# The first gate and value weights ordered behind the first blocks' values, and the whole schedule searched anew

## The chip, the cores and the metric

One core of a Trainium2 chip. The time is the device time of one execution in microseconds, of which the profile's span covers the instructions. The engines go by their profile names: PE (matrix), PEld (its weight loads), ACT (scalar), DVE (vector), POOL (GpSimd) and SP (sync, which here only issues loads and stores).

## The reference, cut to what matters

Sparse attention over four batches, then a gated feed-forward layer over the 3072 rows.

```python
# q, k, v: (4, 8 heads, 768, 64); chunks of 32 keys, the 6 best per row
ub = sum(maximum(q * k_min, q * k_max))        # bound of each chunk
sel = the 6 chunks of largest ub among the causal ones
attn = softmax(where(sel & causal, q @ k.T / 8, -1e9)) @ v
x = attn as (3072, 512)
out = (sigmoid(x @ w_gate) * (x @ w_val)) @ w_out   # 512 -> 1536 -> 512
```

In the first 128 rows of a batch there are at most four causal chunks, so nothing has to be chosen there.

## The kernel before, in words

The rows are cut into eight units of three blocks of 128 rows. Unit 0 holds the first blocks of batches 0, 1 and 2, which need no choice of chunks; the first block of batch 3 goes with unit 2. For every unit u the operations have names:

- `first` (unit 0 and the block of batch 3): loads `kf`, `qf` (two halves each, L575) and `vf` (L570); transposes `kfT`, `qfT` (L648), casts `kf16`, `qf16`; scores `scf` (L685); exponentials `expf` on ACT (L690); the causal mask `cmf` on POOL (L692); products with the values `pvf` (L699); reciprocal and scaling `rzf`, `xf` (L705, L707); transposes `xpsf` (L714) and copies `xTf` into the transposed rows `xT`. The values are cast as `v16_0_0` (batch 0, L612) or `vc_1`, `vc_2`. `vf1` sets the ones column.
- `keys_wide`, `queries_wide` (units 1 and 2): loads `k0..k3`, `q0..q3` (L586), copies `kn`, `qn`, transposes `kT`, `qT` (L734), extremes `kx` (L620), copies `hk`, `hq`, positive parts `qm` (L636 on DVE or POOL, L634 on ACT). Later units take keys and queries in blocks.
- `choose`: bounds `ub` (L835), then on DVE the transposes, the eight largest and the mask that the scores add.
- `attend`: scores `sc` (L896), exponentials (L907), causal mask `cm` on POOL (L913), products with the values `pv` (L929), `rz`, `x`, `xps`, `xT`.
- `ffn`: for each of twelve column blocks a gate product `g` and a value product `v` (four matmuls each, L1078), tanh on ACT (L1087), their product `hg` on DVE (L1091); for units 0 to 3 the output products `o0`, `o1`, `o2` (L1119), copied and stored; units 4 to 7 use seven products of sums (`p`, L1013) instead.

The weights come as nine loads issued on POOL, each a third of a matrix, which convert from 32 to 16 bits:

```python
def weights(i, prio, after):
    lo, hi = 512 * i, 512 * i + 512
    return plan.add(f"wg{i}", {POOL: (760, 760)}, lambda e: nc.gpsimd.dma_start(wg16[:, :, lo:hi], wgs[:, :, lo:hi]),
             reads=after, writes=[("wg", i)], prio=prio, dma=(3000, 2048)), ...   # the same for wv{i}
```

`weights_out` does so for `wo0..wo2` (L557). Gate blocks 0 to 3 need `wg0`, 4 to 7 `wg1`, 8 to 11 `wg2`; the values likewise; `o0` needs `wo0` and so on.

The order of the work is written out. A table ORDER lists all 1826 operations with their engine, found by a search outside the kernel, and a table SLOTS gives each of 991 buffers its place. The kernel walks ORDER and emits each operation on the engine named; each engine then works off its own queue in that order:

```python
for w in ORDER.split():
    name, _, e = w.partition("=")
    op.engine = {"P": PE, "A": ACT, "V": DVE, "G": POOL, "S": SP}[e]
    assert op.engine in op.engines and all(d in done for d, _ in op.deps), name
```

The dependencies in the plan (`reads`, `writes`) bind the search and are asserted here. The waits of the program come from the tiles that an instruction touches.

Of the kernel before, what the change touches and what calls it, by code (L numbers as in the profile page):

```python
# [96 lines left out]
epat0=V ident=G vf1_2=G epat=G v10=G ident16=V kcr0=V kf0_0=S hkp000=A k2_u1=S kn_u1_2=V kT_u1_2=P kx1_u1_2=V hkp011=V vf1_1=G  # L97
hkp001=G kf1_0=S kfT_0=P kf16_0=V kt_u1_2=A hkp010=V hk1_u1_2=V ap0=V hkp100=V qf0_0=S qf1_0=S qfT_0=P qf16_0=A kf1_1=S kf0_1=S
kfT_1=P kf16_1=A scf_0=P expf_0_0=A qf0_1=S qf1_1=S qfT_1=P qf16_1=A scf_1=P k0_u1=S wg0=G expf_0_1=A cmf_0_1=G vf_0=S v16_0_0=G
pvf_0_1=P kx0_u1_2=V rzf_0_1=V xf_0_1=V kn_u1_0=A kT_u1_0=P qf1_2=S kf0_2=S qf0_2=S kf1_2=S kfT_2=P hq0=V kf16_2=V expf_1_0=A  # L100
cmf_1_0=G qfT_2=P qf16_2=A cmf_0_0=G pvf_0_0=P rzf_0_0=V xf_0_0=V vf_1=S vc_1=G xpsf_0_1=P pvf_1_0=P rzf_1_0=V expf_1_1=A
cmf_1_1=G wv0=G scf_2=P expf_2_0=A cmf_2_0=G xTf_0_1=A xpsf_0_0=P xf_1_0=V xpsf_1_0=P kxf0=V pvf_1_1=P rzf_1_1=V xf_1_1=V
xpsf_1_1=P kxf1=V expf_2_1=A kt_u1_0=A vf_2=S cmf_2_1=G vc_2=A pvf_2_1=P rzf_2_1=V xf_2_1=V pvf_2_0=P rzf_2_0=V xf_2_0=V k1_u1=S
kn_u1_1=A kT_u1_1=P xTf_1_0=V xTf_1_1=V xpsf_2_1=P xTf_2_1=V kx1_u1_0=V q0_u1=S qn_u1_0=A qT_u1_0=P xpsf_2_0=P q1_u1=S qn_u1_1=A
qT_u1_1=P q2_u1=S kt_u1_1=A qn_u1_2=A qT_u1_2=P wv1=G wg1=G wv2=G k3_u1=S kn_u1_3=A kT_u1_3=P hk1_u1_0=A xTf_0_0=V qf_u1_1=V
xTf_2_0=A g_u0_2=P qf_u1_0=A qf_u1_2=A hkp110=A q3_u1=S hk0_u1_1=G kcr_f=G hkf0=G hk1_u1_1=G qn_u1_3=G qm_u1_0=A qT_u1_3=P
qm_u1_2=A qf_u1_3=A hk0_u1_2=G kx1_u1_1=V ap1=V kx0_u1_0=V kx0_u1_1=V hq0_u1_1=G wg2=G hq0_u1_2=G qm_u1_1=V kx1_u1_3=V kx0_u1_3=V
kt_u1_3=V g_u0_3=P g_u0_0=P g_u0_1=P hq0_u1_0=V kcr_u1=V v_u0_3=P qm_u1_3=A tanh_u0_2=A tanh_u0_0=A tanh_u0_3=A v_u0_2=P hg_u0_2=V
hkf1=V v_u0_0=P hg_u0_0=V hq0_u1_3=G wo0=G hk0_u1_3=G ub_u1=P ubn0_u1=V ubm0_u1=V mx0_u1=V ubn1_u1=V ap0_u1=V apt0_u1=V
hqm0_u1_0=G wo1=G hkp101=A hk1_u1_3=A hkp111=A tanh_u0_1=A hk0_u1_0=A v_u0_5=P v_u0_4=P v_u0_7=P hg_u0_3=V kcr1=V v_u0_1=P  # L110
hg_u0_1=V hqm0_u1_2=A g_u0_5=P tanh_u0_5=A hg_u0_5=V hq1=V g_u0_7=P tanh_u0_7=A hg_u0_7=V hq1_u1_3=V ubm1_u1=V sc_u1_3_2=P
sc_u1_2_2=P sc_u1_3_1=P exp_u1_3_2=A exp_u1_2_2=A g_u0_4=P tanh_u0_4=A hg_u0_4=V mx1_u1=V ap1_u1=V hq1_u1_1=V apt1_u1=V
sc_u1_0_2=P sc_u1_0_1=P exp_u1_0_2=A exp_u1_0_1=A sc_u1_1_1=P exp_u1_1_1=A sc_u1_2_1=P exp_u1_2_1=A sc_u1_2_0=P sc_u1_1_0=P
hq1_u1_0=G hq1_u1_2=G g_u0_6=P tanh_u0_6=A sc_u1_1_2=P exp_u1_2_0=A cm_u1_2=G wo2=G sc_u1_3_0=P exp_u1_3_0=A sc_u1_0_0=P
exp_u1_0_0=A exp_u1_3_1=A v_u0_8=P v_u0_9=P v_u0_6=P hg_u0_6=V hqm1_u1_0=V g_u0_9=P tanh_u0_9=A g_u0_8=P g_u0_10=P tanh_u0_10=A
g_u0_11=P tanh_u0_11=A exp_u1_1_0=A exp_u1_1_2=A v_u0_10=P hg_u0_10=V o0_u0_0=P v_0_3=S v_0_1=S v16_0_3=G cm_u1_3=G v16_0_1=G
hqm1_u1_2=G v_0_2=S v16_0_2=G pv_u1_2=P hg_u0_9=V pv_u1_3=P rz_u1_1=V x_u1_1=V tanh_u0_8=A hg_u0_8=V sc_u1_4_2=P exp_u1_4_2=A
# [4 lines left out]
o1_u0_0=P o2_u0_0=P k1_u2=S k2_u2=S kn_u2_2=V kT_u2_2=P kx1_u2_2=V kt_u2_2=V q0_u2=S qn_u2_0=A kt_u2_0=A xT_u1_0=A kn_u2_1=A
qT_u2_0=P qf_u2_0=A osb_u0_0=A cm_u1_7=G pv_u1_7=P pv_u1_6=P q3_u2=S qn_u2_3=G qT_u2_3=P rz_u1_3=V x_u1_3=V kT_u2_1=P pv_u1_5=P
cm_u1_4=G pv_u1_4=P kf0_3=S k3_u2=S kn_u2_3=G kT_u2_3=P q1_u2=S qn_u2_1=A hq0_u2_0=G hk1_u2_0=G qm_u2_2=G hq0_u2_2=G xps_u1_3=P
qT_u2_1=P o1_u0_1=P kx0_u2_2=V rz_u1_2=V x_u1_2=V kx1_u2_1=V xps_u1_2=P qf1_3=S kf1_3=S kfT_3=P qm_u2_0=A qf_u2_3=A hq0_u2_3=G
# [1132 lines left out]
```

## Time and profile before

| | us |
|---|---|
| median of 3 runs | 290.59 (290.22 to 292.78) |
| the profiled execution | 291.15 |
| its span | 289.4 |
| PE busy in it | 272.8 |
| DVE, ACT, POOL busy | 213.6, 186.9, 147.0 |

The mean granted clock of PE is 0.982 over the span. A row of the timeline gives start, length, engine, line, operation, what it writes and reads, how many, and in brackets the idle time ahead of it with what ended it. "DMA to landing" is the time from a load's issue to its data being there, lowest, median and highest of the loads asked for.

### The profile page before, as it was taken

What the parts mean: (1) busy time and instruction counts of PE and PEld (TensorE: products, weight loads), DVE (VectorE), ACT (ScalarE), POOL (GpSimd) and SP (SyncE); (2) the same over time, 40 slices, a digit from 0 to 9 for tenths busy, and PEclk for the clock granted to TensorE, in tenths of its full rate; (3) what the DMA queues carried; (4) which work ended last, traced back from release to release, by engine and by line L of the source; (5) the groups of instructions that cost most, each with busy time, mean ns of one, the idle gap of its engine ahead of it and who ended that gap; (6) DMA issues with size and microseconds to landing.
All of it is one profiled execution on the core that took longest, in us unless ns stands there. A gap on an engine that the chain in (4) does not pass through costs nothing.

```text
span 289.4 us, 7287 instructions
## 1 busy us (share of the span) xinstructions
PE 272.8 (94%) x2764; PEld 187.3 (65%) x2764; DVE 213.6 (74%) x613; ACT 186.9 (65%) x394; POOL 147.0 (51%) x233
## 2 busy tenths in 40 slices
PE   2478999999999999999999999999999999999994
...
GB/s 161 199 264 215 211 212 205 174 194 155 182 259 163 104 181 81 91 155 201 219 198 89 37 76 38 2 0 2 2 76 1 0 2 0 111 0 111 0 0 146
DMA packets 123378, 32.70 MB, mean 113 GB/s; under 512 B 111440, under 2 KB 120400, under 8 KB 123344
## 3 DMA queue, kind: packets, MB, share of 16 engines
...
q14 instruction: 13, 0.11, 0.1%
HBM read 30.67 MB, written 6.29 MB: 128 GB/s over the span
## 4 chain that ended last, share of the span: by engine, by line
PE 81%; DMA 8%; DVE 4%; POOL 2%; SPq 1%; issue 1%; ACT 0%; DVEq 0%; POOLq 0%; ACTq 0%
PE v_u L1078 19%; PE g_u L1078 18%; PE sc_u L896 11%; PE o_u L1119 10%; PE p_u L1013 8%; PE pv_u L929 7%; DMA wo<-in_moe_w_out_dram 6%; PE ube_u L835 2%; PE xps_u L956 2%; SPq L575 1%; DMA kf<-in_k_dram 1%; PE kfT L648 1%; DMA kq_u<-in_k_dram 1%; PE qT_u L734 1%; DVE ox L1030 1%
## 5 line engine op out<-in xcount | busy, mean ns | idle before, releaser
L907 ACT ACTIVATE att_u<-sc_u 128x512 f16<-128x512 f32 (+3 forms) x184 | 86.7, 579 | 8.9 <-PE sc_u L896 8.1
L1087 ACT ACTIVATE gate_u<-g_u 128x384 f16<-128x384 f32 x96 | 46.3, 500 | 55.7 <-PE g_u L1078 40.2
L1091 DVE SCALAR_TENSOR_TENSOR hg_u<-gate_u,v_u 128x384 f16<-128x384 f16 x96 | 50.9, 546 | 35.6 <-PE v_u L1078 29.0
L1078 PE MATMUL g_u<-xT_u,wg 128*128 128x384 f16 x384 | 73.7, 328 | 0.7 <-DMA wg<-in_moe_w_gate_dram 0.7
L1078 PE MATMUL v_u<-xT_u,wv 128*128 128x384 f16 x384 | 72.1, 326 | 0.0
L1078 PEld LDWEIGHTS <-wv 128*128 128x128 f16 x384 | 36.6, 98 | 22.7 <-issue 0.5
L1078 PEld LDWEIGHTS <-wg 128*128 128x128 f16 x384 | 36.3, 98 | 23.1 <-DMA wg<-in_moe_w_gate_dram 1.5
L913 POOL TENSOR_SCALAR_AFFINE_SELECT att_u<-att_u 128x384 f16<-128x384 f16 (+1 forms) x56 | 28.3, 510 | 41.1 <-ACT att_u L907 40.3
L1119 PE MATMUL o_u<-wo,hg_u 128*128 128x512 f16 x144 | 34.0, 379 | 0.1
L929 PE MATMUL pv_u<-v,att_u 128*128 128x65 f16 x640 | 26.5, 193 | 0.0
L929 PEld LDWEIGHTS <-att_u 128*128 128x128 f16 x640 | 24.1, 97 | 2.2 <-issue 0.6
L896 PE MATMUL sc_u<-hqe,hke 128*128 128x128 f16 (+2 forms) x220 | 24.3, 243 | 0.2 <-POOL hqe L411 0.2
L896 PE MATMUL sc_u<-hqo,hko 128*128 128x128 f16 (+2 forms) x220 | 24.3, 243 | 0.0
L1119 PEld LDWEIGHTS <-hg_u 128*128 128x128 f16 x144 | 13.8, 98 | 14.4 <-DMA wo<-in_moe_w_out_dram 0.5
L896 PEld LDWEIGHTS <-hke 128*128 128x128 f16 x220 | 16.4, 98 | 5.1 <-ACT osb_u L1128 0.6
L896 PEld LDWEIGHTS <-hko 128*128 128x128 f16 x220 | 16.5, 98 | 3.9
L612 POOL CAST v<-v 128x512 f16<-128x512 f32 x23 | 14.5, 637 | 3.1 <-PE pv_u L929 2.3
L948 DVE TENSOR_TENSOR x_u<-pv_u,rz_u 128x384 f16<-128x384 f32 (+1 forms) x28 | 14.7, 529 | 0.7
L1030 DVE SCALAR_TENSOR_TENSOR sw<-p_u,sw 128x256 f32<-128x256 f32 (+1 forms) x20 | 10.6, 531 | 5.8 <-PE p_u L1013 3.4
L1000 POOL TENSOR_TENSOR sw<-hg_u 128x256 f16<-128x256 f16 x5 | 3.3, 669 | 18.4 <-DVE hg_u L1091 18.4
L858 DVE MAX8 mx_u<-ubn_u 128x8 f32<-128x8 f32 (+16 forms) x152 | 12.4, 162 | 0.2
L636 POOL TENSOR_SCALAR qm_u<-qf_u 128x768 f32<-128x768 f32 (+2 forms) x6 | 11.4, 1894 | 0.3
...
## 6 DMA issues: line engine op xcount, KB each, us to landing
...
wo<-in_moe_w_out_dram POOLq DMA_DIRECT2D x3, 512.0 KB, 13.5
```

The lines of the kernel that those rows point to most:

```text
L612: plan.add(f"v16_{b}_{ib}", {POOL: pool(H * D)}, lambda e: nc.gpsimd.tensor_copy(v16[b % 2][:, ib, :, 0:D], at(t)), reads=[t], writes=[("v ...
L896: nc.tensor.matmul(at(t)[:, o:o + 128 * m], hk[b % 2][e_][:, p, 128 * jb:128 * jb + 128], hq[u.side][e_][:, p, 128 * x:128 * (x + m)], sta ...
L907: plan.add(f"exp_{u.name}_{h}_{y}", {ACT: act(n)}, lambda e, t=t, att=att, b0=b0, n=n: nc.scalar.activation(at(att)[:, b0:b0 + n], at(t), ...
L913: nc.gpsimd.affine_select(out=dv, in_=dv, compare_op=ALU.is_ge, fill=0.0, base=0, pattern=[[0, u.m], [1, 128]], channel_multiplier=-1)
L929: nc.tensor.matmul(at(pv)[:, last, x, :], at(att)[:, c:c + 128], v16[b % 2][:, jb, h, :], start=(jb == 0), stop=(jb == ib))
L948: plan.add(f"x_{u.name}_{p}", {DVE: dve(u.t)}, lambda e: nc.vector.tensor_tensor(at(x_).rearrange("p a (e d) -> p e a d", e=2), at(pv)[:, ...
L1013: nc.tensor.matmul(at(to)[:, side], a(j)[:, i], b(j)[:, i], start=j == i == 0, stop=j == 2 and i == 1)
L1030: plan.add(f"{p}_{name}", {DVE: dve(256 * n)}, lambda e: nc.vector.scalar_tensor_tensor(four()[:, lo], at(src) if n == 1 else at(src)[:, 0 ...
L1078: nc.tensor.matmul(at(t), w16[:, c, 128 * fb:128 * fb + 128], at(u.xt)[:, c, :], start=(c == 0), stop=(c == 3))
L1087: plan.add(f"tanh_{u.name}_{fb}", {ACT: act(T)}, lambda e, g=g, gate=gate: nc.scalar.activation(at(gate), at(g), AF.Tanh, scale=0.5), read ...
L1091: plan.add(f"hg_{u.name}_{fb}", {DVE: dve(T)}, lambda e, w_=w_, gate=gate, hg=hg, fb=fb: nc.vector.scalar_tensor_tensor(at(hg)[:, fb % 2], ...
L1119: nc.tensor.matmul(at(o), at(hgs[fc // 2])[:, fc % 2, 128 * tb:128 * tb + 128], wo16[:, fc, lo:hi], start=(fc == 0), stop=(fc == NFB - 1))
```

## The change

The first gate and value weights get one more dependency in the plan, and ORDER and SLOTS are searched anew, over three sets of durations.

```diff
 for i in range(3):
-    weights(i, -0.9 + 0.2 * i, [])
+    weights(i, -0.9 + 0.2 * i, [raw_f[2]["v"]] if i == 0 else [])
```

`raw_f[2]["v"]` is the tile that `vf_2` loads. 139 of 1826 operations change their engine (POOL keeps 227 and SP 108, DVE goes from 467 to 469, ACT from 393 to 391), and 728 of 991 buffers their place. The queues' beginnings, taken out of ORDER:

```diff
 SP
-kf0_0 k2_u1 kf1_0 qf0_0 qf1_0 kf1_1 kf0_1 qf0_1 qf1_1 k0_u1 vf_0 qf1_2 kf0_2 qf0_2 kf1_2 vf_1 vf_2 k1_u1 q0_u1 q1_u1 q2_u1 k3_u1 q3_u1 v_0_3 v_0_1 v_0_2
+k2_u1 kf1_0 kf0_0 qf0_0 kf0_1 qf1_0 qf0_1 kf1_1 qf1_1 vf_0 qf1_2 qf0_2 kf1_2 kf0_2 k0_u1 vf_1 vf_2 k1_u1 q1_u1 q2_u1 q0_u1 k3_u1 q3_u1 v_0_3 v_0_1 v_0_2
 POOL
-ident vf1_2 epat v10 vf1_1 hkp001 wg0 cmf_0_1 v16_0_0 cmf_1_0 cmf_0_0 vc_1 cmf_1_1 wv0 cmf_2_0 cmf_2_1 wv1 wg1 wv2 hk0_u1_1 kcr_f hkf0 hk1_u1_1 qn_u1_3 hk0_u1_2 hq0_u1_1 wg2 hq0_u1_2 hq0_u1_3 wo0
+ident v10 epat hkp000 v16_0_0 cmf_0_0 cmf_0_1 hk1_u1_2 cmf_1_0 kn_u1_0 vf1_1 vf1_2 cmf_1_1 wg0 wv0 cmf_2_0 cmf_2_1 qn_u1_1 wv1 kn_u1_3 qn_u1_3 wg1 kcr_f wv2 qm_u1_2 hk0_u1_2 qm_u1_3 wg2 hqm0_u1_0 wo0
 ACT
-hkp000 kt_u1_2 qf16_0 kf16_1 expf_0_0 qf16_1 expf_0_1 kn_u1_0 expf_1_0 qf16_2 expf_1_1 expf_2_0 xTf_0_1 expf_2_1
+kn_u1_2 hkp011 hkp100 expf_0_0 expf_0_1 qf16_1 expf_1_0 expf_1_1 qf16_2 vc_1 kf16_2 vc_2 expf_2_0 expf_2_1
 PE
-kT_u1_2 kfT_0 qfT_0 kfT_1 scf_0 qfT_1 scf_1 pvf_0_1 kT_u1_0 kfT_2 qfT_2 pvf_0_0 xpsf_0_1 pvf_1_0 scf_2 xpsf_0_0 xpsf_1_0 pvf_1_1 xpsf_1_1 pvf_2_1 pvf_2_0 kT_u1_1 xpsf_2_1 qT_u1_0 xpsf_2_0 qT_u1_1 qT_u1_2 kT_u1_3 g_u0_2 qT_u1_3 g_u0_3 g_u0_0 g_u0_1
+kT_u1_2 kfT_0 qfT_0 kfT_1 scf_0 qfT_1 scf_1 pvf_0_0 qfT_2 pvf_0_1 kfT_2 kT_u1_0 pvf_1_0 xpsf_0_1 pvf_1_1 scf_2 xpsf_0_0 xpsf_1_0 xpsf_1_1 pvf_2_0 pvf_2_1 kT_u1_1 xpsf_2_0 qT_u1_2 xpsf_2_1 kT_u1_3 qT_u1_1 qT_u1_3 qT_u1_0 g_u0_3 g_u0_0 g_u0_2 g_u0_1
```

Further on, PE's order keeps its milestones (the bounds `ub_u2`, `ub_u3`, `ub_u4` and `ub_u7` have as many instructions ahead as before), with changes in between; the positive parts `qm_u6_0` and `qm_u6_2` go from ACT to POOL; the store `out_u3_2` goes from its old place to one between `out_u7_0` and `out_u7_1`.

More of the change, by code (lines that the diff above doesn't have):

```diff
@@ L96 @@
 ORDER = """
[L97 to L117, printed above, removed]
@@ L122 @@
[L122 to L125, printed above, removed]
@@ L246 @@
-p5_u67=P p5z_u67=P sw3_u67_0=G sw3_u67_2=V p3_u67=P c11_u67=V u4_u67=V p3z_u67=P c12_u67=V out_u67_0=S p7_u67=P p7z_u67=P
-c22_u67=V out_u67_b1=S p4_u67=P p4z_u67=P c21_u67=V out_u67_1=S
+ident=G v10=G ident16=V k2_u1=S kn_u1_2=A kT_u1_2=P epat0=V epat=G hkp010=V hkp011=A hkp100=A kcr0=V hkp000=G kf1_0=S kf0_0=S
+kfT_0=P qf0_0=S kf0_1=S kf16_0=V kxf0=V qf1_0=S qfT_0=P qf0_1=S kf1_1=S kfT_1=P kx0_u1_2=V qf16_0=V scf_0=P expf_0_0=A kf16_1=V
+expf_0_1=A qf1_1=S qfT_1=P hkp001=V kt_u1_2=V qf16_1=A scf_1=P expf_1_0=A vf_0=S v16_0_0=G cmf_0_0=G pvf_0_0=P rzf_0_0=V xf_0_0=V
@@ new lines @@
+kxf1=V expf_1_1=A qf1_2=S qf0_2=S qfT_2=P qf16_2=A cmf_0_1=G pvf_0_1=P hk1_u1_2=G rzf_0_1=V xf_0_1=V kf1_2=S kf0_2=S kfT_2=P
+cmf_1_0=G k0_u1=S kn_u1_0=G kT_u1_0=P vf_1=S vf1_1=G vc_1=A pvf_1_0=P rzf_1_0=V xf_1_0=V vf1_2=G cmf_1_1=G xpsf_0_1=P pvf_1_1=P
+rzf_1_1=V xf_1_1=V kf16_2=A scf_2=P xpsf_0_0=P xpsf_1_0=P ap0=V kx1_u1_2=V vf_2=S vc_2=A wg0=G wv0=G xpsf_1_1=P expf_2_0=A
+cmf_2_0=G pvf_2_0=P ap1=V rzf_2_0=V kt_u1_0=V xf_2_0=V expf_2_1=A cmf_2_1=G pvf_2_1=P k1_u1=S q1_u1=S q2_u1=S qn_u1_2=A xTf_0_1=A
@@ new lines @@
+kn_u1_1=A kT_u1_1=P q0_u1=S k3_u1=S q3_u1=S qn_u1_1=G wv1=G kn_u1_3=G xTf_1_0=A xTf_0_0=A hkp110=A qn_u1_3=G xpsf_2_0=P qT_u1_2=P
+hq1=V rzf_2_1=V xf_2_1=V xTf_1_1=V kx1_u1_0=V hk0_u1_0=V xpsf_2_1=P xTf_2_1=V kx1_u1_1=V wg1=G qn_u1_0=A xTf_2_0=A kt_u1_1=A
+kcr_f=G wv2=G qf_u1_2=V qm_u1_2=G kT_u1_3=P qT_u1_1=P qf_u1_1=A hq1_u1_1=A kx0_u1_3=V qT_u1_3=P qf_u1_3=V kx1_u1_3=V qT_u1_0=P
+qf_u1_0=V hk0_u1_2=G qm_u1_3=G kx0_u1_1=V kx0_u1_0=V kcr_u1=V hk1_u1_1=A qm_u1_1=A qm_u1_0=A wg2=G kt_u1_3=V hk1_u1_3=V hkf0=V
@@ new lines @@
+kt_3_3=V qf0_u7_1=V o0_u3_1=P xps_u5_0=P o1_u3_0=P o1_u3_1=P exp_u5_6_1=A o2_u3_1=P osb_u3_1=A out_u3_1=S sc_u5_6_2=P ub_u6=P
+ubn1_u6=V ubn0_u6=V ubm1_u6=V mx1_u6=V ubm0_u6=V mx0_u6=V exp_u5_6_2=A hq0_u6_0=A g_u4_0=P qm_u7_2=A hk0_3_3=A pv_u5_4=P o2_u3_0=P
+tanh_u4_0=A osb_u3_0=A out_u3_0=S g_u4_1=P tanh_u4_1=A exp_u5_5_2=A v_u4_1=P o0_u3_2=P o1_u3_2=P o2_u3_2=P osb_u3_2=A qm_u7_0=G
+ub_u7=P v16_3_2=G cm_u5_6=G ap0_u6=V hq0_u6_2=V ap1_u6=V xT_u5_0=A apt0_u6=V apt1_u6=V hqm1_u6_2=A hqm0_u6_2=G sc_u6_3_1=P
@@ new lines @@
+tanh_u7_11=A hg_u7_11=V sw0_u7_2=V p1_u7=P p1z_u7=P out_u6_0=S p1s_u7=A p7z_u7=P p2_u7=P p2z_u7=P p4z_u7=P sw1_u7_2=V p5_u7=P
+p5z_u7=P p6_u7=P p6z_u7=P held_u6_1=V sw3_u7_2=V p2_u67=P sw0_u67_2=V sw1_u67_2=V held_u6_5=V p2z_u67=P sw3_u7_1=G p3_u7=P
+p3z_u7=P p1_u67=P p1z_u67=P p1s_u67=A c11_u7=V u4_u7=V c12_u7=V out_u7_0=S out_u3_2=S c22_u7=V c21_u7=V out_u7_1=S p6_u67=P
+p6z_u67=P p5_u67=P p5z_u67=P sw3_u67_0=G sw2_u67_0=G p3_u67=P sw3_u67_2=V p3z_u67=P c11_u67=V u4_u67=V c12_u67=V out_u67_0=S
@@ L248 @@
+sw2_u67_2=G p7_u67=P p7z_u67=P c22_u67=V out_u67_b1=S p4_u67=P p4z_u67=P c21_u67=V out_u67_1=S
 """
 SLOTS = """
-epat:0 kf_0:0 qf_0:1 vf_0:4 kf_1:2 qf_1:3 vf_1:1 kf_2:0 qf_2:5 vf_2:2 kq_u1:0 v_0_1:4 v_0_2:0 v_0_3:3 kfT_0:1 kf16_0:3 kx_f:1
-qfT_0:2 qf16_0:4 scf_0_0:4 scf_0_1:5 attf_0_0:1 pvf_0_0:5 rzf_0_0:1 xf_0_0:1 xpsf_0_0:5 xT_u0:0 attf_0_1:3 pvf_0_1:3 rzf_0_1:0
-xf_0_1:0 xpsf_0_1:7 kfT_1:3 kf16_1:5 qfT_1:6 qf16_1:6 vh_1:2 scf_1_0:7 scf_1_1:2 attf_1_0:2 pvf_1_0:3 rzf_1_0:0 xf_1_0:2
-xpsf_1_0:2 attf_1_1:1 pvf_1_1:3 rzf_1_1:1 xf_1_1:0 xpsf_1_1:6 kfT_2:6 kf16_2:4 qfT_2:0 qf16_2:5 vh_2:0 scf_2_0:6 scf_2_1:0
@@ L328 @@
-v_u7_5:5 g_u7_6:6 gate_u7_6:2 hg_u7_3:6 v_u7_6:7 g_u7_7:2 gate_u7_7:1 v_u7_7:1 g_u7_8:3 gate_u7_8:0 hg_u7_4:0 v_u7_8:1 g_u7_9:2
-gate_u7_9:2 v_u7_9:7 g_u7_10:4 gate_u7_10:3 hg_u7_5:2 v_u7_10:3 g_u7_11:2 gate_u7_11:1 v_u7_11:4 p1_u7:5 p26_u7:0 p5_u7:1 p3_u7:2
-p7_u7:6 p4_u7:7 p1_u67:3 p26_u67:4 p5_u67:5 p3_u67:0 p7_u67:1 p4_u67:3
+epat:0 kf_0:0 qf_0:1 vf_0:4 kf_1:2 qf_1:3 vf_1:1 kf_2:0 qf_2:5 vf_2:2 kq_u1:0 v_0_1:4 v_0_2:5 v_0_3:3 kfT_0:1 kf16_0:1 kx_f:0
+qfT_0:2 qf16_0:2 scf_0_0:4 scf_0_1:5 attf_0_0:1 pvf_0_0:3 rzf_0_0:0 xf_0_0:0 xpsf_0_0:6 xT_u0:0 attf_0_1:2 pvf_0_1:5 rzf_0_1:1
```

404 lines of the change are left out of this document (208 added, 196 removed).

## The prediction

> **What bounds the kernel now.** I read the page first: its span, the busy shares and the forty slices. Then the table by stage, the timeline of the first 27 us, the landings of single loads, and the chain that ended last.
>
> ```profile
> span 289.4 us, 7287 instructions
> PE 272.8 (94%) x2764; PEld 187.3 (65%) x2764; DVE 213.6 (74%) x613; ACT 186.9 (65%) x394; POOL 147.0 (51%) x233
> PE   2478999999999999999999999999999999999994
> ```
>
> PE is busy for 272.8 of 289.4 us. The slices put nearly all of the other 16.6 us at the two ends. The table by stage says where (columns: stretch, length, then busy time and instructions of PE, weight load, DVE, ACT and POOL, the granted clock, DMA share, GB/s):
>
> ```profile
> 8.00:13.00 5.00, 2.58 (x23) 1.67 (x22) 1.91 (x5) 3.49 (x7) 0.63 (x1) 1.00 1.18 214
> 13.00:15.00 2.00, 0.00 (x0) 0.00 (x0) 0.00 (x0) 0.00 (x0) 0.53 (x1) 0.61 0.59 132
> 15.00:24.00 9.00, 6.94 (x61) 5.14 (x60) 5.74 (x18) 5.41 (x13) 6.28 (x11) 0.69 1.07 267
> 24.00:32.00 8.00, 8.00 (x58) 5.46 (x64) 6.80 (x18) 7.86 (x15) 6.40 (x13) 0.81 1.21 205
> 42.30:43.00 0.70, 0.06 (x1) 0.06 (x2) 0.62 (x2) 0.00 (x0) 0.70 (x2) 1.00 1.28 225
> 60.00:87.20 27.20, 26.95 (x310) 18.47 (x310) 25.08 (x67) 23.50 (x52) 16.33 (x29) 1.00 1.06 199
> 174.20:240.00 65.80, 65.80 (x777) 49.78 (x775) 45.98 (x122) 43.16 (x92) 34.25 (x54) 1.00 0.04 14
> 280.00:289.40 9.40, 5.64 (x52) 4.80 (x50) 5.70 (x12) 0.00 (x0) 2.52 (x4) 1.00 0.31 112
> ```
>
> From 13 to 15 us PE does nothing at all. From 43 us to the tail it hardly pauses, so a later stage can lose time but hardly win any: what can be won lies before 54 us. Until then the DMA engines are full (share 1.0 to 1.3) with one exception, the same 13 to 15 us. What stands there:
>
> ```profile
> 5.62 0.74 SPq L586 DMA_DIRECT2D kq_u<-in_k_dram  x1
> 5.69 0.99 POOL L551 DMA_DIRECT2D wg<-in_moe_w_gate_dram  x1
> 6.40 0.47 SPq L570 DMA_DIRECT2D vf<-in_v_dram  x1
> 14.47 0.61 POOL L612 CAST v<-vf 128x512 f16<-128x512 f32 x1 [2.40 <-DMA vf<-in_v_dram]
> 15.14 0.38 PE L699 MATMUL pvf<-v,attf 128*128 128x65 f16 x4 [3.89 <-POOL v L612]
> 20.16 0.78 POOL L552 DMA_DIRECT2D wv<-in_moe_w_val_dram  x1
> 26.05 1.33 PE L1078 MATMUL g_u<-xT_u,wg 128*128 128x384 f16 x4
> ```
>
> The first gate weights (wg0) are issued at 5.69, just ahead of the first block's values (vf_0, 6.40). PE then waits 3.89 us for these values, and the whole chain of the first blocks to the first gate product (26.05) stands behind them. The landings of single loads, asked by tile, in this order: vf_0 (issued 6.40), vf_1 (13.97), vf_2 (14.52), wg0 (5.69), wv0 (20.16), wo2 (41.51):
>
> ```profile
> DMA to landing us min/median/max: 8.0/8.0/8.0
> DMA to landing us min/median/max: 3.2/3.2/3.2
> DMA to landing us min/median/max: 3.6/3.6/3.6
> DMA to landing us min/median/max: 8.1/8.1/8.1
> DMA to landing us min/median/max: 8.6/8.6/8.6
> DMA to landing us min/median/max: 11.8/11.8/11.8
> ```
>
> The same 256 KB take 3.2 to 3.6 us when POOL's queue is empty and 8.0 beside wg0. And the weights come in a steady row once they run: wv0 lands at 28.8, wo2, seven chunks later, at 53.3, so one chunk takes 24.5/7 = 3.5 us while SP's loads run beside it.
>
> **The change part by part.** *The wait itself.* In the built program wg0's issue carries no wait for vf_2. The new dependency binds the search alone; on the chip wg0 and wv0 simply stand later in POOL's queue, behind the fourth causal mask (cmf_1_1). So what sets their time is when POOL gets there.
>
> *vf_0.* It goes from eleventh to tenth place in SP's order, since k0_u1 (5.62, 0.74 us) moves behind it; its issue comes at about 5.8. Bounds for the landing: 5.8 + 3.2 = 9.0, and 14.4 as now. Nothing of POOL's queue runs beside it then, as with vf_1 and vf_2, so I take 9.6 (3.6 and a little more). The PE wait of 3.89 us then shrinks to what the score chain leaves: in the new order of ACT expf_0_1 stands ahead of qf16_1, so scf_1 goes from 10.85 to about 11.2 and pvf_0_0 starts near 12, 3 us earlier than 15.14.
>
> *POOL to wg0.* The rows:
>
> ```profile
> 11.44 0.63 POOL L692 TENSOR_SCALAR_AFFINE_SELECT attf<-attf 128x512 f16<-128x512 f16 x1 [4.76 <-ACT attf L690]
> 24.35 0.54 POOL L411 COPY hke<-kt_u 64x384 f16<-64x384 f16 x1
> 26.23 0.50 POOL L411 COPY qn_u<-kq_u 128x384 f32<-128x384 f32 x1
> 3.94 0.28 POOL L674 MEMSET vh<- 128x8 f16 x1
> 10.70 0.60 ACT L690 ACTIVATE attf<-scf 128x512 f16<-128x512 f32 x1
> 10.85 0.40 PE L685 MATMUL scf<-qf,kf 64*128 64x128 f16 x8 [0.67 <-ACT qf L407]
> ```
>
> From vf_0's landing POOL does one cast (0.61), four masks (4 x 0.63), one key copy (0.54), kn_u1_0 (0.50, moved here from ACT) and two memsets (2 x 0.28): 4.7 us, to 14.3. The third mask waits some 0.3 us for its exponential (scf_1 at 11.2, 0.6 to its end, one exponential of 0.60). So wg0 is issued at 14.6, 8.9 us later than now, and wv0 about 1 us behind, 4.5 us *earlier* than now. Bounds: 13.5 and 18 (the third rival).
>
> *The weights.* The first chunk of a row took 8.1 and 8.6 us; 8.35 puts wg0 at 22.95. Then 3.5 us each, in POOL's order wv0, wv1, wg1, wv2, wg2, wo0, wo1, wo2: wv0 26.5, wg2 40.5, wo0 44.0, wo2 51.0. Against now (28.8, 42.9 = 27.59 + 15.3, 46.4, 53.3) that is 2.3 to 2.4 us earlier each. POOL reaches the later issues long before their turn, as now (wo0 is issued 17.16 us ahead of its landing, chain below). By the bounds of the spacing and of the issue, wo2 lies between 49 and 54.5.
>
> The Trainium skill gives a DMA issued from POOL 2.0 us and its bytes at 436 GB/s (DMA: Bandwidth & Descriptors, section Anatomy of one DMA); by that wg0 (512 KB written) would land 3.2 us after its issue and no gate product would wait for weights, an estimate that leads to the second rival's time. The trace disagrees so far: the shortest of nine weight loads took 8.1 us.
>
> *The gates.* Now the last pvf_2 stands at 22.24 and the first gate at 26.05, 3.8 us.
>
> ```profile
> 22.24 0.43 PE L699 MATMUL pvf<-vh,attf 128*128 128x65 f16 x8 [0.64 <-POOL attf L692]
> 29.27 17.16 DMA wo<-in_moe_w_out_dram
> 46.47 1.04 PE o_u L1119 x4
> 52.91 1.73 PE o_u L1119 x8
> ```
>
> In the new order POOL issues wg0 and wv0 (0.99 + 0.78) between cmf_1_1 and the last two masks: 14.6 + 1.8 + 1.3 = 17.7 for the last pvf_2; plus 3.8, plus one q transpose more that now stands behind the first gate (0.5): 22.0. That is ahead of wg0 (22.95), so wg0 sets the first gate: 26.05 becomes 22.95, 3.1 earlier. The lower clock (0.69 and 0.81 above) may stay or go: the first gate's four matmuls took 1.33 us at 26.05, and at the full clock it would be about half; the waits for the following chunks absorb that.
>
> *From the first gate to wo2.* PE's orders hold 237 instructions now and 235 then between the first gate and o2_u0_0, so the stretch is as long, except for its waits. The chain has PE waiting for wo0 (46.47), the table 0.64 us for wg2 (42.3 to 43), and o2_u0_0, the second half of the x8 row, starts at 53.6, only 0.3 behind wo2. PE by itself would be there at 22.95 + 27.5 - 0.7 = 49.8; wo2 at 51.0 holds it. So 53.6 becomes 51.0: **2.6 us earlier**.
>
> *From there to the end* 139 operations change engine and most buffers, but PE's places stay: ub_u2 has 416 instructions ahead in both, ub_u3 720, ub_u4 1036, ub_u7 1671. ACT and DVE trade two operations. I cost this at nothing: PE covers it, being busy 65.80 of 65.80 us from 174 on. Without that cover one moved copy costs its 0.50 to 0.54 us. out_u3_2's store moves into the tail between out_u7_0 and out_u7_1, where the DMA share is 0.31; at most its one issue (0.47 for vf_0's) reaches the end.
>
> *The sum.* 53.6 - 51.0 = 2.6 us. The profiled execution took 291.15 us for its 289.4 of span; 2.6 off gives 288.5 and a span of 286.8. The median of the runs is 290.59, so **288.0 us**. By its bounds alone (wg0's issue 13.5 to 16, spacing 3.4 to 3.6, a lost copy or two) 286.6 to 289.4.
>
> **The rivals.** *Weights never awaited* (chance 0.17). If chunks pass faster with the DMA engines never pausing at 13 to 15 us, the transposed values set the first gate: 22.0, 4.05 us earlier, and the waits for wg2 and wo0 (0.7) go too: 290.6 - 4.7 = 285.9. For it: the DMA share falls to 0.59 in that gap, so there is room. Against it: seven chunks in a row at 3.5 us. By the rule of DMA: Bandwidth & Descriptors in the Trainium skill, above, it would go this way.
>
> *POOL comes late to wg0* (0.15), the slower side. kn_u1_0 now stands on POOL ahead of wg0 and needs k0_u1, SP's fifteenth load. Now the fifteenth lands at 16.25:
>
> ```profile
> 12.28 3.97 DMA kf<-in_k_dram
> ```
>
> If it does again, kn_u1_0, the memsets and cmf_1_1 (0.50 + 0.56 + 0.63) put wg0 at 18.0, wg0's landing at 26.35 and wo2 at 54.4: 0.8 us later than now, 291.4. It decides from an issue at 17.2 on (17.2 + 8.35 + 28 = 53.6). Against it: wg0 itself is what slowed these loads (8.0 against 3.2 to 3.6 us).
>
> *A copy in the body uncovers PE* (0.18). The largest price: unit 6's two positive parts go from ACT to POOL.
>
> ```profile
> L636 POOL TENSOR_SCALAR qm_u<-qf_u 128x768 f32<-128x768 f32 x4 | 8.7, 2176 | 0.2
> L634 ACT ACTIVATE qm_u<-qf_u 128x768 f32<-128x768 f32 x4 | 3.4, 856 | 0.0
> ```
>
> From qm_u6_2 to ub_u6 PE has about 5.8 us of work in hand and POOL 3.6, so 2.2 to spare. If both (4.4) fall into it, 2.2 us are lost: 290.2. For it: DVE is busy 25.08 of 27.20 us in such a stretch and its queues have little air. Against it: POOL is idle there for 40% of the time. Several such gaps would pass 293.
>
> **How the numbers follow.** The forecast has 0.50. A change of 1% (2.9 us) is about what a measurement of this kernel can tell from none. Of the forecast's 0.50 some 0.23 lies beyond 2.9 us; with the second case's 0.17 that makes faster 0.40. Slower by over 1% needs several gaps at once: 0.11. The rest is 0.49. The range 285.8 to 291.4 holds both outer rivals' times.
>
> **What would show it.** wg0's issue at 14.6 and its landing near 23; vf_0's cast near 9.6 instead of 14.47; no empty stretch at 13 to 15; the first gate at 23; waits of PE for wg, wv or wo between 23 and 51; o2_u0_0 at 51.0; PE busy without gaps from there on, and a tail as now. It is wrong if wg0 is issued after 17, if chunks follow at well under 3.5 us, or if PE shows new waits after 54.

## The result and the profile after

The changed kernel takes 288.74 us (median of 13 runs, 287.76 to 290.44) against 291.60 us for the kernel before (13 runs, 289.65 to 292.78). The ratio of the means is 0.9916, 95% interval 0.9890 to 0.9943: 2.4 us faster, where 290.59 to 288.0 (2.6 us) was predicted. The profiled execution has a span of 286.6 us; the prediction said 286.8. In three of the four experiments below that hold SP's loads, the runs of one kernel fall into two groups some 4 us apart, and while their ratios compare mainly the faster group (spans of 288.0 to 289.6 us), all three profiles (292.6 to 294.1 us) show the slower one, so that no trace shows how the faster ones load their values.

The page of the changed kernel, its span, busy shares and the slices of PE and of the granted clock:

```profile
span 286.6 us, 7277 instructions
PE 272.8 (95%) x2764; PEld 186.3 (65%) x2764; DVE 212.3 (74%) x615; ACT 186.9 (65%) x392; POOL 148.2 (52%) x233
PE   3878999999999999999999999999999999999994
PEclk9999999999999999999999999999999999999999
```

PE is busy for the same 272.8 us; the span lost 2.8 us of idling. In the slices the second one, 7 to 14 us, goes from 4 tenths to 8. The table by stage, same stretches and columns as before:

```profile
8.00:13.00 5.00, 4.12 (x32) 3.12 (x33) 2.79 (x6) 2.47 (x5) 2.44 (x5) 1.00 1.03 241
13.00:15.00 2.00, 2.00 (x14) 1.88 (x13) 1.28 (x4) 1.80 (x4) 2.00 (x6) 1.00 1.03 263
15.00:24.00 9.00, 6.45 (x60) 4.41 (x59) 7.69 (x24) 7.71 (x17) 6.77 (x12) 1.00 1.09 208
60.00:87.20 27.20, 27.20 (x300) 18.54 (x299) 24.13 (x62) 23.67 (x50) 20.31 (x35) 1.00 1.04 188
174.20:240.00 65.80, 65.80 (x731) 49.77 (x729) 42.37 (x124) 41.03 (x89) 29.84 (x47) 1.00 0.05 18
```

The empty stretch from 13 to 15 us is full. The later stages were full before and are full now. The timeline shows the steps that the prediction named:

```profile
9.55 0.61 POOL L612 CAST v<-vf 128x512 f16<-128x512 f32 x1 [3.11 <-DMA vf<-in_v_dram]
12.09 0.34 PE L699 MATMUL pvf<-v,attf 128*128 128x65 f16 x3
14.59 0.99 POOL L551 DMA_DIRECT2D wg<-in_moe_w_gate_dram  x1
15.58 0.76 POOL L552 DMA_DIRECT2D wv<-in_moe_w_val_dram  x1
18.40 0.30 PE L699 MATMUL pvf<-vh,attf 128*128 128x65 f16 x4 [0.29 <-POOL attf L692]
21.98 0.87 PE L734 MATMUL qT_u<-ident,qn_u 128*128 128x128 f32 x6 [1.04 <-POOL qn_u L411]
23.30 0.50 PE L1078 MATMUL g_u<-xT_u,wg 128*128 128x384 f16 x2 [0.45 <-DMA wg<-in_moe_w_gate_dram]
37.79 0.77 POOL L557 DMA_DIRECT2D wo<-in_moe_w_out_dram  x1
51.01 0.59 PE L1119 MATMUL o_u<-wo,hg_u 128*128 128x512 f16 x2 [0.31 <-DMA wo<-in_moe_w_out_dram]
57.10 0.40 PE L835 MATMUL ube_u<-qf_u,kcr 64*32 64x256 f32 x1
```

The landings of single loads: vf_0 (issued 5.64), wg0 (14.59), wv0 (15.58), wo2 (37.79):

```profile
DMA to landing us min/median/max: 3.8/3.8/3.8
DMA to landing us min/median/max: 8.7/8.7/8.7
DMA to landing us min/median/max: 11.0/11.0/11.0
DMA to landing us min/median/max: 13.2/13.2/13.2
```

So vf_0 lands at 9.4 instead of 14.4, wg0 at 23.3, wv0 at 26.6, wo2 at 51.0. Seven chunks after wv0 it is 24.4 us later: 3.49 us each, as before. The bounds `ub_u2` begin at 57.1 instead of 59.98:

```profile
59.98 0.40 PE L835 MATMUL ube_u<-qf_u,kcr 64*32 64x256 f32 x1
```

From there to the end of the span it is 229.4 and 229.5 us (289.4 - 59.98 and 286.6 - 57.1), and in every other kernel run here within 0.2 us of that, but for one (230.2). All that the change does to the time is done before 57 us.

### The profile page after: what moved, and what is told of

It is laid out like the page before. It is cut to its first block, busy times and chain, and to the rows that moved or that the text cites. A ratio compares the mean times of both kernels' runs of the same rounds, so it can differ in the third digit from the quotient of the medians.

```text
span 286.6 us, 7277 instructions
## 1 busy us (share of the span) xinstructions
PE 272.8 (95%) x2764; PEld 186.3 (65%) x2764; DVE 212.3 (74%) x615; ACT 186.9 (65%) x392; POOL 148.2 (52%) x233
## 3 DMA queue, kind: packets, MB, share of 16 engines
q1 hardware_dynamic: 118592, 27.53, 45.9%
## 4 chain that ended last, share of the span: by engine, by line
PE 81%; DMA 12%; SPq 2%; POOL 1%; DVE 1%; issue 1%; DVEq 0%
PE g_u L1078 19%; PE v_u L1078 19%; PE sc_u L896 11%; PE o_u L1119 10%; PE p_u L1013 9%; PE pv_u L929 6%; DMA wo<-in_moe_w_out_dram 5%; DMA wg<-in_moe_w_gate_dram 4%; PE ube_u L835 2%; DMA kq_u<-in_q_dram 2%; PE xps_u L956 1%; SPq L586 1%; DMA kf<-in_k_dram 1%; SPq L575 1%; DVE ox L1030 1%
## 5 line engine op out<-in xcount | busy, mean ns | idle before, releaser
L1087 ACT ACTIVATE gate_u<-g_u 128x384 f16<-128x384 f32 x96 | 47.1, 503 | 58.4 <-PE g_u L1078 53.1
L1078 PE MATMUL g_u<-xT_u,wg 128*128 128x384 f16 x384 | 73.2, 326 | 0.9 <-DMA wg<-in_moe_w_gate_dram 0.9
L1078 PE MATMUL v_u<-xT_u,wv 128*128 128x384 f16 x384 | 72.5, 326 | 0.0
L1078 PEld LDWEIGHTS <-wg 128*128 128x128 f16 x384 | 36.0, 98 | 24.5 <-DMA wg<-in_moe_w_gate_dram 1.8
L1078 PEld LDWEIGHTS <-wv 128*128 128x128 f16 x384 | 36.2, 98 | 22.9 <-issue 0.5
L913 POOL TENSOR_SCALAR_AFFINE_SELECT att_u<-att_u 128x384 f16<-128x384 f16 (+1 forms) x56 | 28.2, 514 | 36.1 <-ACT att_u L907 30.6
L1119 PE MATMUL o_u<-wo,hg_u 128*128 128x512 f16 x144 | 34.6, 379 | 0.4 <-DMA wo<-in_moe_w_out_dram 0.3
L929 PE MATMUL pv_u<-v,att_u 128*128 128x65 f16 x640 | 26.6, 193 | 0.0
L896 PE MATMUL sc_u<-hqo,hko 128*128 128x128 f16 (+2 forms) x220 | 25.7, 243 | 0.0
L896 PE MATMUL sc_u<-hqe,hke 128*128 128x128 f16 (+2 forms) x220 | 25.1, 243 | 0.0
L612 POOL CAST v<-v 128x512 f16<-128x512 f32 x23 | 13.7, 613 | 15.0 <-DMA v<-in_v_dram 14.7
L636 POOL TENSOR_SCALAR qm_u<-qf_u 128x768 f32<-128x768 f32 (+3 forms) x10 | 16.2, 1617 | 3.3 <-PE ubo_u L835 2.0
L1128 ACT ACTIVATE osb_u<-o_u 128x512 f32<-128x512 f32 x10 | 6.0, 596 | 10.1 <-PE o_u L1119 10.1
```

The lines of the kernel that those rows point to most:

```text
L612: plan.add(f"v16_{b}_{ib}", {POOL: pool(H * D)}, lambda e: nc.gpsimd.tensor_copy(v16[b % 2][:, ib, :, 0:D], at(t)), reads=[t], writes=[("v ...
L636: (nc.vector if e == DVE else nc.gpsimd).tensor_scalar_max(o, i, 0.0)
L896: nc.tensor.matmul(at(t)[:, o:o + 128 * m], hk[b % 2][e_][:, p, 128 * jb:128 * jb + 128], hq[u.side][e_][:, p, 128 * x:128 * (x + m)], sta ...
L913: nc.gpsimd.affine_select(out=dv, in_=dv, compare_op=ALU.is_ge, fill=0.0, base=0, pattern=[[0, u.m], [1, 128]], channel_multiplier=-1)
L929: nc.tensor.matmul(at(pv)[:, last, x, :], at(att)[:, c:c + 128], v16[b % 2][:, jb, h, :], start=(jb == 0), stop=(jb == ib))
L1078: nc.tensor.matmul(at(t), w16[:, c, 128 * fb:128 * fb + 128], at(u.xt)[:, c, :], start=(c == 0), stop=(c == 3))
```

## The experiments

Each was timed beside the kernel before. Since ORDER is wrapped otherwise in them, their lines of code stand some lines further down (L1081 for L1078).

**Undoing the one part.** The changed kernel, with wg0 alone back at the front of POOL's queue (and the plan's new dependency taken out, which would forbid it):

```diff
-... epat hkp000 v16_0_0 cmf_0_0 ... vf1_2 cmf_1_1 wg0 wv0 cmf_2_0
+... epat hkp000 wg0 v16_0_0 cmf_0_0 ... vf1_2 cmf_1_1 wv0 cmf_2_0
```

> The changed kernel with wg0 alone put back to the front of POOL's queue (right behind hkp000, so issued at about 6.4 us). My theory (the 512 KB of wg0 push back SP's first-block loads): vf_0 lands near 14 us again instead of 9.4, PE stands idle again between about 12 and 15 us, the first gate product moves from 23.3 to about 25, and the time rises by 1.2 to 2.5 us over the changed kernel (290 to 291). Rival (the newly searched order of the other operations brings the gain, wg0's place does not): 288.7, no change, although vf_0 is late.

Measured: ratio to the kernel before 1.0134 (1.0093 to 1.0174), median 295.98 us, span 292.7. So it is some 6 us slower than the changed kernel, far more than I expected, and by another way. Lines of its timeline, then PE's two longest waits between 10 and 60 us:

```profile
6.39 0.99 POOL L554 DMA_DIRECT2D wg<-in_moe_w_gate_dram  x1
10.54 5.28 SPq L573 DMA_DIRECT2D vf<-in_v_dram  x2
18.35 0.78 POOL L555 DMA_DIRECT2D wv<-in_moe_w_val_dram  x1
18.72 0.47 SPq L589 DMA_DIRECT2D kq_u<-in_k_dram  x1
...
PE qfT L651 <- DMA qf<-in_q_dram: 4.0, 1, 4.0
PE kT_u L737 <- POOL kn_u L414: 2.7, 1, 2.7
```

vf_0 was issued at 5.67, ahead of wg0, and landed at 9.9 unhurt, so this run does not test what wg0 does to vf_0. What wg0 hurts is what SP issues from then on: PE waits 4.0 us for a half of qf_2, vf_1 lands at 18.0 (13.8 in the changed kernel). SP itself gets stuck (two issues take 5.28 us), so the loads k3 and q3 of unit 1 are issued only at 18.7 and 19.2, into the company of wv0 (18.35), and take 7.8 and 8.2 us; the key copy that waits for k3 costs PE another 2.7. The first gate stands at 29.8. Here wg0 and then wv0 each delay the loads issued beside them.

**The one part alone.** The kernel before, with wg0 moved to just ahead of wv0; then with both one mask earlier:

```diff
-... hkp001 wg0 cmf_0_1 v16_0_0 cmf_1_0 cmf_0_0 vc_1 cmf_1_1 wv0 cmf_2_0
+... hkp001 cmf_0_1 v16_0_0 cmf_1_0 cmf_0_0 vc_1 cmf_1_1 wg0 wv0 cmf_2_0    # first run
+... hkp001 cmf_0_1 v16_0_0 cmf_1_0 cmf_0_0 vc_1 wg0 wv0 cmf_1_1 cmf_2_0    # second run
```

> The kernel before with one operation moved: wg0 from its early place to just ahead of wv0, behind cmf_1_1. Nothing else of the searched order. My theory: vf_0 lands near 9.5, the empty stretch at 13 to 15 goes, wg0 is issued near 16 and lands near 24.5, the row of weights ends with wo2 near 52 instead of 53.3, and 1.3 to 2.5 us of the 2.8 are won by this one move (289 to 290.3). Rival (the order as a whole has to be searched anew for it to pay): no change or slower, 291.6 or more.

> The kernel before with wg0 and wv0 moved to just behind the third value copy's neighbour vc_1 on POOL, ahead of the mask cmf_1_1 (in the run with wg0 alone moved, vc_1 ended at 15.0 or sooner and cmf_1_1 waited for its exponential until 16.2): wg0 is issued at about 14.5 instead of 16.8, wv0 at 15.5 instead of 17.8. Nothing else of the searched order. Theory (when wg0 is issued, behind the first block's loads, is all that counts): wg0 lands near 23, wo2 near 51, ub_u2 2 to 2.8 us ahead of the kernel before, and the time is that of the changed kernel within 0.5 us (288.7 to 289.3). Rival (the rest of the searched order is needed, since the masks, value copies and transposes set the first gate in the old order): first gate at 24 or later, time 290 to 290.7 as with wg0 alone moved.

Measured: the first 0.9976 (0.9954 to 0.9997), span 288.8: 0.7 us, less than expected. The second 0.9918 (0.9893 to 0.9943), span 287.0: the whole gain of the changed kernel (0.9916), with two entries of ORDER moved and nothing searched. First run, then second, POOL's issue of wg0, its landing and the first gate:

```profile
16.80 0.99 POOL L554 DMA_DIRECT2D wg<-in_moe_w_gate_dram  x1
DMA to landing us min/median/max: 7.6/7.6/7.6
24.47 0.50 PE L1081 MATMUL g_u<-xT_u,wg 128*128 128x384 f16 x1 [0.33 <-DMA wg<-in_moe_w_gate_dram]
...
14.36 1.00 POOL L554 DMA_DIRECT2D wg<-in_moe_w_gate_dram  x1
DMA to landing us min/median/max: 9.0/9.0/9.0
23.36 0.50 PE L1081 MATMUL g_u<-xT_u,wg 128*128 128x384 f16 x1
```

In the first run POOL waits 1.77 us for the exponential of cmf_1_1 before it comes to wg0, so the whole row of weights runs 1.9 us later (wo2 at 52.8 against 51.0). In the second wg0 is issued at 14.4 and the row ends at 51.1. In both, with wg0 out of their way, the loads vf_0 to vf_2 take 3.4 to 4.5 us (vf_0 took 8.0 in the kernel before); the first run shows that this alone brings little. What counts is the time at which the row of weights begins; the 139 changed engines and 728 changed places brought nothing that can be measured here.

**The row moved either way.** The changed kernel, with wg0 and wv0 4 us later (behind the query copy qn_u1_1) and 3 us earlier (behind the mask cmf_0_1; the plan's new dependency is taken out for this):

```diff
-... cmf_0_0 cmf_0_1 hk1_u1_2 ... cmf_1_1 wg0 wv0 cmf_2_0 cmf_2_1 qn_u1_1 wv1
+... cmf_0_0 cmf_0_1 hk1_u1_2 ... cmf_1_1 cmf_2_0 cmf_2_1 qn_u1_1 wg0 wv0 wv1    # later
+... cmf_0_0 cmf_0_1 wg0 wv0 hk1_u1_2 ... cmf_1_1 cmf_2_0 cmf_2_1 qn_u1_1 wv1    # earlier
```

> The changed kernel with wg0 and wv0 moved 4.2 us later on POOL (behind qn_u1_1, so issued at about 18.8 instead of 14.6). My theory (the row of weights sets the time up to wo2): wo2 lands and o2_u0_0 starts 3 to 4.2 us later (54 to 55.2), the time rises by as much (291.7 to 292.9). Rival (weights are hidden, the transposes set the first gate): wo2's delay shows in no wait of PE, 288.7 to 289.2.

> The changed kernel with wg0 and wv0 moved 2.8 us earlier on POOL (behind cmf_0_1, so issued at about 11.8, past vf_0 but ahead of vf_1's landing). My theory: wg0 lands near 20.5 and wo2 near 48.3, so that the transposes (22.9 in the changed kernel) and PE's own work set the stretch: 287.5 to 288.5, a gain of up to 1.2 us. Rival (the weights push back vf_1, vf_2 and the loads of unit 1 as wg0 pushed back vf_0): those loads land 2 to 4 us later, the first gate stands at 25 or later, and the time is 289.5 to 291.

Measured, later: 1.0000 (0.9977 to 1.0024), so the gain is gone; wo2 lands at 53.7 and the span is 2.9 us longer. That is a little under the 3 to 4.2 expected, since wg0 now runs nearly alone and takes 6.6 us instead of 8.7. In its profile PE waits only 0.8 us for weights: its first 16 gate products take 5.26 us, at a granted clock of 0.64 from 23 to 33 us, against 2.77 us at 1.00 in the changed kernel, so this profile alone does not part the row from the clock. Earlier: 1.0015 (0.9989 to 1.0041), and there my theory fell and the rival held, with a median (292.1) a little beyond its 291. Later first, then two lines of the earlier one, of its chain and of PE's waits:

```profile
18.54 1.00 POOL L554 DMA_DIRECT2D wg<-in_moe_w_gate_dram  x1
DMA to landing us min/median/max: 6.6/6.6/6.6
PE g_u L1081 <- DMA wg<-in_moe_w_gate_dram: 0.8, 1, 0.8
...
13.67 9.49 DMA kq_u<-in_q_dram
PE kT_u L737 <- ACT kn_u L410: 5.6, 1, 5.6
```

Issued at 11.65, wg0 lands at 20.3, but a query load of unit 1 now takes 9.49 us (4.1 in the changed kernel). ACT's copy of it waits, and a key copy that stands behind it in ACT's queue costs PE 5.6 us at kT. The first gate comes at 28.2. Of the places tried, 14.4 to 14.6 is the best: earlier, the loads of unit 1 pay; later, the weights. Where the loads of unit 1 do not pay, the end of the row and the median time go together: wo2 at 53.7 (later run, 291.5 us), 53.3 (kernel before, 291.6), 52.8 and 51.1 (the one-part runs, 290.7 and 288.9) and 51.0 (changed kernel, 288.7).

**Holding SP's loads back.** Is a chunk every 3.4 us its own rate, or the price of SP's loads beside it? A first pair of runs named wg1 or wv0 in the plan as what the value load v_0_3 reads.

```diff
-            writes=[t], prio=prio, dma=(1150, 256))
+            reads=[("wg", 1)] if (b, ib) == (0, 3) else [], writes=[t], prio=prio, dma=(1150, 256))
```

> The changed kernel with one wait more: SP's load v_0_3 waits until wg1 has landed, and with it everything behind it on SP's queue (v_0_1, v_0_2 and the twelve 128 KB loads after them). In the changed kernel v_0_3 is issued at 15.45 and these loads share the DMA engines with the weights. Theory A (the 3.46 us between chunks come from that sharing, and the weights still set the end of the start): wv0, wv1 and wg1 follow at 3 us or less, wo2 lands 1 to 3 us earlier, PE's waits for wg1, wo0 and wo2 (about 1 us) go, o2_u0_0 starts near 50, and the time is 287.7 to 288.7. Rival B (3.46 us is a chunk's own rate): the spacing stays at 3.4 to 3.5 and the time at 288.7. Rival C (the held loads come too late for the second unit, about 2.3 MB from 31 us on): ub_u2 moves behind 58 and the time is 289.5 or more.

> As in the run with the wait for wg1, but v_0_3 waits for wv0 only, the second chunk (26.6 us in the changed kernel), so that only two chunks run without SP's loads beside them and the held loads start some 7 us sooner. Theory A: wv0 follows wg0 by 3 us or less, the later chunks as now; wo2 0.5 to 1 us earlier, time 288.2 to 288.8. Rival B: no change of the spacing, 288.7. Rival C: 289 or more.

Measured: 0.9899 (0.9850 to 0.9949) and 0.9939 (0.9911 to 0.9968). Nothing was held: v_0_3 was issued at 15.07 in the first of them, with wg1 landing at 34.2. As with the change itself, a dependency named in the plan orders the table and makes no wait. The two are the changed kernel again, operation for operation, and show how far its executions differ: spans of 288.4 and 287.4, at clocks of 0.982 and 0.994.

The second try puts a real load on SP that touches the chunk, so that SP waits for it, ahead of v_0_3:

```diff
+    held_ = lone("held_", [128, 4])
...
+    plan.add("hold", {SP: (450, 450)}, lambda e: nc.sync.dma_start(held_, wg16[:, 0, 512:516]),
+             reads=[("wg", 1)], writes=["held_"], prio=0.3, dma=(100, 8))
```

The runs differ in the chunk: wv0, wg1, wg0, and wg0 in the kernel of the second one-part run.

> The changed kernel with one small load more on SP, ahead of v_0_3: 8 bytes of each of 128 rows copied from wv0's place in SBUF to a tile that nobody reads, so that SP waits there until wv0 has landed (26.6 us), and v_0_3 and all loads of the second unit behind it. (The two runs that named the chunk in the plan alone added no wait: v_0_3 was issued at 15 us in them as in the changed kernel.) Theory A (chunks are 3.46 us apart because SP's loads share the DMA engines): wv0 follows wg0 by 2.8 us or less, wo2 lands 0.5 to 2 us earlier, PE's waits for weights (about 1 us) shrink, time 287.7 to 288.6. Rival B (3.46 is a chunk's own rate): spacing 3.3 to 3.5, time 288.7. Rival C (the held loads come too late for the second unit): ub_u2 behind 58, time 289.5 or more.

> As in the run that holds SP's loads until wv0, but until wg1, the fourth chunk (33.3 us in the changed kernel). Theory A: four chunks at 2.8 us or less, wg1 lands near 31 and wo2 1 to 3 us earlier; no wait of PE for weights. Rival B: spacing 3.3 to 3.5 throughout. Rival C, likelier here than with wv0: v_0_1 to v_0_3 and the twelve 128 KB loads, 2.3 MB from 31 to 33 us on, come too late; ub_u2 behind 58, 289.5 or more.

> The changed kernel with SP's loads held only until wg0 has landed (23.3 us), by the same small copy on SP, 8 bytes of each row of wg0's place. Holding them until wv0 or wg1 brought the chunks to 2.5 us apart, but the first block's values v_0_1 and v_0_2 landed at 44 to 47.7 us and PE waited 6 us for them. Theory (the DMA engines are full from 8 to 54 us, so what the weights gain the values lose): wg0 lands 0.5 to 0.9 us earlier, first gate near 22.4, v_0_2 lands at 43 to 45 instead of 41.7, and PE, which reaches pv_u1 near 42 in this order, waits 1 to 3 us for it: 289 to 291. Rival (there is slack in the values, only a long hold hurts): no wait at pv_u1, first gate 0.9 us earlier, 287.8 to 288.5.

> The kernel before with wg0 and wv0 behind vc_1 (which equalled the changed kernel), and with the same hold until wg0 has landed. Its order has the first attention products of unit 1 2 us later (44.8 against 42.7), so v_0_2 has more air. Theory of full DMA engines: v_0_2 lands at 44 to 45.5, a wait of 0 to 1.5 us, time 288 to 289.7, no better than without the hold within 0.3%. Rival (slack): first gate 22.4, no wait at pv_u1, 287.8 to 288.3, a version that beats the changed kernel.

Measured, in this order: 1.0017 (0.9974 to 1.0060), 0.9985 (0.9952 to 1.0018), 1.0018 (0.9979 to 1.0056) and 1.0109 (1.0075 to 1.0142); medians 295.69, 294.17, 295.39 and 294.48 us. None beats the changed kernel; by these ratios all lose most or all of its gain. The hold until wg1 shows both halves of it: issue and landing of wv0, then of wg2, four chunks on; then PE's wait:

```profile
15.18 0.76 POOL L556 DMA_DIRECT2D wv<-in_moe_w_val_dram  x1
DMA to landing us min/median/max: 10.2/10.2/10.2
24.68 0.81 POOL L555 DMA_DIRECT2D wg<-in_moe_w_gate_dram  x1
DMA to landing us min/median/max: 10.9/10.9/10.9
...
PE pv_u L933 <- POOL v L616: 6.5, 2, 5.7
```

With SP silent until 34 us the chunks follow each other every 2.55 us ((35.6 - 25.4)/4), against 3.36 in the changed kernel over the same five. So theory A held for the spacing, and wo2 landed at 45.6. But rival C held for the time: the values v_0_1 and v_0_2 came at 46.1 and 47.0 instead of 34.8 and 41.6, and in the profiled execution PE stood 6.5 us before the first attention products of unit 1. The short hold until wg0 shows the same wait in its profile (6.6 us). For these three kernels the lost time is traced in the profiled executions alone. In the fourth, whose six runs lie together (293.50 to 296.19 us) and take some 5.6 us more than without the hold, the profile has the wait too:

```profile
PE pv_u L933 <- POOL v L616: 6.4, 1, 6.4
```

**Whose turn it is.** The last run asks how the two queues share. The transfer view of the changed kernel, 26 to 44 us, where both have work all the time (packets, MB, share of the engines):

```profile
q0 software_dynamic: 2768, 2.75, 89.9%
q1 hardware_dynamic: 2767, 0.82, 31.0%
```

POOL's and SP's queues moved the same number of packets, to one. The page has POOL's packets of the whole span:

```profile
q0 software_dynamic: 4752, 4.72, 9.8%
```

That is 528 for each of the nine chunks. A value load (rows of 256 bytes, 1024 of them) needs about as many packets as two chunks, and two chunks is how long each took: the three landed at 28.2, 34.8 and 41.6. If so, half as long rows in the weights must double their packets and let a value load land every 4.2 us instead of 6.9, at the same bytes:

```diff
+        def halves(to, of):
+            for m in ((lo, hi),) if i == 0 else ((lo, lo + 256), (lo + 256, hi)):
+                nc.gpsimd.dma_start(to[:, :, m[0]:m[1]], of[:, :, m[0]:m[1]])
...
-lambda e: nc.gpsimd.dma_start(wg16[:, :, lo:hi], wgs[:, :, lo:hi])
+lambda e: halves(wg16, wgs)     # the same for wv
```

> The changed kernel with four of the nine weight loads (wv1, wg1, wv2, wg2) each issued as two loads of half the columns; the other five stay whole. The bytes are the same, but a row of a load is half as long, so that each half should again have some 500 packets. In the changed kernel 2768 packets of POOL's queue and 2767 of SP's were moved between 26 and 44 us, one for one, a value load (1024 rows of 256 bytes) landed every 6.9 us, in the time of two chunks, and a chunk took 3.36 us beside SP's loads and 2.56 without. Theory T (the two queues take turns packet by packet): a half chunk takes half of 2.56 and the 0.8 us of SP's packets, so 2.1 us, two halves 4.2 instead of 3.36; a value load lands every 4.2 us instead of 6.9 while these chunks run, v_0_2 near 37 instead of 41.7, wg2 near 43 instead of 40.1; wo2 lands some 1 to 2.5 us later than 51 since SP's later loads have moved up, time 288.7 to 291. Rival S (the queues share by bytes or by engine time): chunks 3.4 us, a value load every 6.9 us, as in the changed kernel, time 288.7.

Measured: 1.0124 (1.0092 to 1.0157), median 295.53 us. POOL's packets of the whole span on the page, then the same view and PE's two longest waits:

```profile
q0 software_dynamic: 6864, 4.72, 10.6%
q0 software_dynamic: 4152, 2.12, 84.5%
q1 hardware_dynamic: 4275, 1.36, 48.2%
PE g_u L1084 <- DMA wg<-in_moe_w_gate_dram: 2.3, 1, 2.3
PE kT_u L740 <- POOL kn_u L414: 2.3, 1, 2.3
```

6864 is 528 for each of five whole chunks and eight halves. Again the queues go nearly one for one, now with 2.12 MB instead of 2.75 for the weights and 1.36 instead of 0.82 for SP. The value loads landed at 29.5, 33.7 and 38.5, 4.2 and 4.7 us apart, and the half chunks every 2.1 to 2.5. Theory T held, rival S fell. The weights paid more than I reckoned: wg2 at 45.9 (43 expected), PE waited 2.3 us for it, and as long for a key copy, wo2 landed at 56.4, and the time lies well above the 291 expected at most. The rule is in the Trainium skill, DMA: Bandwidth & Descriptors, section Queues, rings and completion order: a DMA engine goes round the queues that have work, packet by packet. Both traces agree in the counts. A packet is a group of descriptors on that page, while the packets that the profile counts are about one to a row (528 for the 512 rows of a chunk), so these traces do not show how many rows an engine takes at one turn.

## Why the prediction was right

*The wait itself.* Right. vf_2 was issued at 10.38 and landed 4.3 us later, near 14.7, and POOL issued wg0 at 14.59, with no idle time ahead of it: nothing waited. The two runs with a dependency in the plan alone show the same.

*vf_0, POOL to wg0, the weights, the chain.* 9.6 was 9.4; 12 was 12.09; wg0's issue at 14.6 was 14.59, from a sum of six rows of the profile before. That it met to the hundredth is luck: POOL waited 0.95 us for exponentials ahead of its masks (0.37 and 0.58) where 0.3 was reckoned, and its two memsets, put at 0.56, took 0.18. The landing of wg0 at 22.95 was 23.3 (8.7 us for the first chunk where 8.35 was taken), wo2 at 51.0 was 51.0, o2_u0_0 51.0 was 51.01, and `ub_u2` came 2.9 us earlier where 2.6 was said. The later run (the gain gone with the row) and the second of the one-part runs (the gain whole) show that the row of weights is the term that counts.

*The gates: right in the result, wrong in a term.* The last pvf_2 was put at 17.7 and stood at 18.4; the transposes were to be done at 22.0 and ended at 22.85, only 0.45 us ahead of wg0. What the sum had left out is that wg0 and wv0 slow SP's last loads too: q3 of unit 1, issued at 14.88, landed 6.5 us later (4.2 us in the run with the weights 4 us later), and POOL's copy of it let PE wait for 1.04 us (21.98 above). I counted what wg0 no longer does to vf_0 and not what it now does to q3. Three us earlier this term becomes the bound, as the run showed.

*The body at nothing.* Right to the tenth: 229.5 us from `ub_u2` on, with or without the 139 changed engines. The positive parts of unit 6 on POOL uncovered nothing.

*The rivals.* PE's waits for weights in the changed kernel, 13 to 60 us:

```profile
PE g_u L1078 <- DMA wg<-in_moe_w_gate_dram: 0.9, 2, 0.5
PE o_u L1119 <- DMA wo<-in_moe_w_out_dram: 0.3, 1, 0.3
```

The weights were awaited, so the second way fell. The price of 3.2 us for a weight load, worked out from DMA: Bandwidth & Descriptors of the Trainium skill, section Anatomy of one DMA, is not met by any of the runs; the shortest first chunk took 6.6 us. It had counted 512 KB written; the 1 MB of 32-bit rows read at that page's 436 GB/s would be an estimate of 2.4 us, and the spacing with SP silent was 2.55. POOL was not late, since the fifteenth load landed at 12.8.

*The clock: a step that did not hold.* The prediction left a lower clock in the start to the waits for the chunks, which would absorb it. In the copy with the dependency on wg1, at clocks of 0.77 and 0.72 (table at the end), they did not: the first 16 gate products took 4.73 us instead of 2.77, wo2 landed at 51.4, and PE came to o2_u0_0 only at about 52.8. At that clock PE's own work, not the weights, is the bound. The timed runs agree. Of the 30 runs of the changed kernel and its two copies that the ratios use, the 7 with a mean clock below 0.985 took 290.4 us on average, the 4 at 0.996 and above 288.0; for the 101 runs of the kernel before beside the experiments the same two averages are 291.6 and 291.5. So the gain was about 1.2 us at the lower clocks and 3.5 at the full one.

*The size.* 2.6 us were predicted from the trace, 2.8 stand between the two profiles, and 2.4 by the ratio of the runs, which is a mix of clocks from 0.980 to 1.000. The profile before had a clock of 0.982, that after of 1.000, so that the sum met the profile so closely is in part the draw of that execution.
